# First q of block 0 through SP's hardware queue, k ahead of q in block 0, and state decay and transposes issued a block ahead

## The chip, the cores and the metric

The kernel runs on one core of a Trainium2 chip. The metric is the device time of one execution in microseconds (us), lower is better. Six runs of the kernel before gave a median of 243.56 us (242.32 to 244.79). One more execution was recorded by the hardware profiler; all times inside the kernel come from that trace. A core has these engines, each with its own instruction stream: TensorE (PE, matmuls; PEld is its weight load), Vector (DVE), Scalar (ACT), GpSimd (POOL) and Sync (SP). An engine runs its stream in order. DMAs are issued from a stream too: those of SP and Scalar through a hardware queue, those of GpSimd through a software queue that can also change the type of the data.

## The reference

Two stages. The first is attention with a decaying state. q, k and v have 4 batches, 8 heads, 768 positions and 64 values per head; `lam` has one decay factor per head, from 0.97 to 0.99. The second is a gated layer on the 3072 x 512 result.

```python
intra = np.einsum('bhic,bhjc->bhij', qb, kb) * Dmask[None]      # lam ** (i - j), below the diagonal
intra = np.einsum('bhij,bhjd->bhid', intra, vb)
inter = np.einsum('bhid,bhde->bhie', qb * lam_pow[None], kv_state)
out[:, :, sl] = intra + inter
kv_state = lam_block * kv_state + np.einsum('bhsd,bhse->bhde', kb * rev_pow, vb)
...
gate = 1.0 / (1.0 + np.exp(-(x @ w_gate)))
return (gate * (x @ w_val)) @ w_out                             # 512 -> 1536 -> 512
```

All inputs and the output are fp32.

## The kernel before

The positions are cut into NSTEP = 6 blocks of 128, and each block holds all 4 batches (numbered b) and 8 heads as 4 head pairs (hp, with u for one head of the pair). A block passes through attention and then through the gated layer, with its 4 x 128 = 512 tokens as the columns of a matmul.

The pieces of attention, for block n:

- `load` (L71) brings q, k or v of some batches with a DMA from GpSimd's queue that casts fp32 to bf16. A piece of one head and one position is 64 values: 256 bytes in HBM, 128 bytes after the cast.
- q and k are transposed. Blocks 0 and 1 do that on PE (`piece_tq0`, `piece_tk0`, `piece_t`); blocks 2 to 5 by two DMA transposes on SP's queue (`transpose_by_dma`, L147; results QR and KR). Vector multiplies the transposed q with the decay factors and gives QS (L162, L177, L186).
- `piece_s` (L206): the scores sp = k q on PE, for each batch in two banks of PSUM. `piece_m` (L214): Vector multiplies them with the mask and gives MT, one instruction for each u.
- `piece_a`: the output op, from the state Sb (L220, not for block 0) and from MT and v (L227); Scalar casts it to XT (L234), the input of the gated layer.
- `make_kd` (L238): GpSimd scales k by the reversed decay. `piece_c` (L246): PE multiplies that with v for the new part of the state, GpSimd scales the old state (sd, L251, four instructions for a block), and Vector adds both into Sb (L257, L259).

The gated layer: `piece_gv` does one tile of 128 of the 1536 columns: four matmuls to gp (L270), a sigmoid on Scalar (L273), four matmuls to vp (L276), and a product on Vector (L279, ht). `piece_gvh` does it for half of the tokens. `piece_po` does the last matrix for 128 tokens: 12 matmuls (L302), a copy by Scalar to ob (L305, four buffers), and a store of 256 KB on SP's queue (L306).

The order of the work is written out by hand: `manual_schedule` keeps for each engine the order in which the program issues its instructions, from L55 on. So the place of a call in the program sets what stands ahead of it in each engine's stream and queue. In the head, GpSimd issues q and k of batches 0 and 1, some index patterns, then q, k and v of the rest, and then the first three weight pairs. `idle` puts matmuls on zeros between the pieces of block 0. From L378 on, the pieces of attention of the next block lie between the tiles of the gated layer of the present one. The loads of block 2 and later come by `fetch` (L365): load, `make_kd` and the two transposes at one place, for block 2 after `t(1, 1)`, for block n + 1 at the start of iteration n of the loop at L422. Block 0's and block 1's `piece_po`, with their stores, stand ahead of that loop.

Buffers that matter: q, k and v have four each (blocks 0 to 3 take one each), kd two, sd four, QR and KR two, PSUM five banks for attention and three for the gated layer.

Of the kernel before, what the change touches and what calls it, by code (L numbers as in the profile page):

```python
# [8 lines left out]
FP32 = mybir.dt.float32  # L9
BF16 = mybir.dt.bfloat16  # L10
AF = mybir.ActivationFunctionType
ALU = mybir.AluOpType
# [4 lines left out]
def kernel(  # L17
# [11 lines left out]
    nc = tc.nc  # L29

    B, H, S, D = q.shape
    C = 128
    NSTEP = S // C
    HP = H // 2
# [22 lines left out]


    lam_bc = const.tile([128, H], FP32, tag="lam_bc")
    nc.sync.dma_start(out=lam_bc, in_=lam.partition_broadcast(128))  # L60

    WG = const.tile([128, NMT, DFF], BF16, tag="WG")
    WV = const.tile([128, NMT, DFF], BF16, tag="WV")
# [7 lines left out]
    def load(n, what, b0, b1):  # L71
        sl = slice(n * C, (n + 1) * C)
        for c in what:
            lst, src = {"q": (Q, q), "k": (K, k), "v": (V, v)}[c]
            if n not in lst:
                lst[n] = qkv.tile([128, B, H, D], BF16, tag=c + "b", name=c + "b")
            t = lst[n]
            nc.gpsimd.dma_start(  # L78
                out=t[:, b0:b1],
                in_=src[b0:b1, :, sl, :].rearrange("b h s d -> s (b h) d"))  # L80

    def load_gv(i, w):
        fs = slice(i * w, (i + 1) * w)
        nc.gpsimd.dma_start(out=WG[:, :, fs], in_=wg_r[:, :, fs])
        nc.gpsimd.dma_start(out=WV[:, :, fs], in_=wv_r[:, :, fs])
# [12 lines left out]
    nc.vector.memset(ident, 0.0)  # L98
    nc.vector.memset(tri, 0.0)

    load(0, "q", 0, 2)
    load(0, "k", 0, 2)
    for i, base in enumerate((-1, C - 1)):
        nc.gpsimd.iota(jn[:, i:i + 1], pattern=[[0, 1]], base=base, channel_multiplier=-1,
# [3 lines left out]
                   allow_small_or_imprecise_dtypes=True)  # L108
    nc.gpsimd.affine_select(out=tri, in_=tri, compare_op=ALU.is_gt, fill=1.0, base=0,
                            pattern=[[-1, C]], channel_multiplier=1)  # L110
    load(0, "q", 2, 4)
    load(0, "k", 2, 4)
    load(0, "v", 0, 2)
    load(0, "v", 2, 4)

    lnl = const.tile([128, H], FP32, tag="lnl")
    nc.scalar.activation(lnl, lam_bc, AF.Ln)
# [7 lines left out]
    for hp in range(HP):  # L125
# [4 lines left out]
    nc.scalar.activation(dec, lnp, AF.Exp, scale=float(C))  # L130
    nc.scalar.preload_act_table_set("sigmoid_and_others")
    mask = const.tile([128, 2, HP, C], FP32, tag="mask")
    nc.vector.tensor_tensor(out=mask, in0=tri.unsqueeze(1).unsqueeze(1).to_broadcast([128, 2, HP, C]),
                            in1=pk.rearrange("p (g u) -> p u g", u=2).unsqueeze(3).to_broadcast([128, 2, HP, C]),
                            op=ALU.mult)

    def idle(n, cols=TCH):
        w = ps_ff.tile([128, TCH], FP32, name="wm", tag="ff")
        for i in range(n):
            nc.tensor.matmul(w[:, :cols], lhsT=zero[:, :128], rhs=zero[:, :cols], start=True, stop=True,  # L140
                             skip_group_check=True)
# [14 lines left out]
    def piece_tq0(bp):  # L156
        tq = ps_at.tile([128, 2, HP, C], BF16, name="tq", tag="ps")
        for i in range(2):
            for hp in range(HP):
                nc.tensor.transpose(tq[:, i, hp, :], Q[0][:, 2 * bp + i, 2 * hp:2 * hp + 2, :], ident)  # L160
        QS[0, bp] = trsb.tile([128, 2, HP, C], BF16, tag="QS", name="QS")
        nc.vector.tensor_tensor(out=QS[0, bp], in0=tq,  # L162
                                in1=lamq.unsqueeze(1).to_broadcast([128, 2, HP, C]), op=ALU.mult)

    def piece_tk0(bp):
        tk = ps_at.tile([128, 2, HP, C], BF16, name="tk", tag="ps")
        for i in range(2):
            for hp in range(HP):
                nc.tensor.transpose(tk[:, i, hp, :], K[0][:, 2 * bp + i, 2 * hp:2 * hp + 2, :], ident)
        KS[0, bp] = trsb.tile([128, 2, HP, C], BF16, tag="KS", name="KS")  # L170
        for i in range(2):
            nc.scalar.copy(KS[0, bp][:, i], tk[:, i])
# [25 lines left out]
    def piece_s(n, bs):  # L198

        for b in bs:  # L200
# [7 lines left out]
                                     start=(hp == 0), stop=(hp == HP - 1), skip_group_check=True)  # L208
            SP[n, b] = sp

    def piece_m(n, b):
        MT[n, b] = mtp.tile([128, 2, HP, C], BF16, tag="MT", name="MT")
        for u in range(2):
            nc.vector.tensor_tensor(out=MT[n, b][:, u], in0=SP[n, b][u], in1=mask[:, u], op=ALU.mult)  # L214

    def piece_a(n, bs):
        for b in bs:
            OP[n, b] = ps_at.tile([128, HP, C], FP32, name="op", tag="ps")
            for hp in range(HP if n > 0 else 0):
                nc.tensor.matmul(OP[n, b][:, hp, :], lhsT=Sb[:, b, hp, :],  # L220
                                 rhs=QS[n, b // 2][:, b % 2, hp, :],
                                 start=(hp == 0), stop=False, skip_group_check=True)
        for b in bs:
            for hp in range(HP):
                for u in range(2):
                    us = slice(u * 64, (u + 1) * 64)
                    nc.tensor.matmul(OP[n, b][us, hp, :], lhsT=V[n][:, b, 2 * hp + u, :],  # L227
                                     rhs=MT[n, b][:, u, hp, :],
                                     start=(n == 0 and hp == 0), stop=(hp == HP - 1),
                                     skip_group_check=True)  # L230
        if n not in XT:
            XT[n] = xtp.tile([128, NMT, B, C], BF16, tag="XT", name="XT")
        for b in bs:
            nc.scalar.copy(XT[n][:, :, b, :], OP[n, b])  # L234

    def make_kd(n):
        KD[n] = kdp.tile([128, B, H, D], BF16, tag="kd", name="kd")
        nc.gpsimd.tensor_tensor(  # L238
            out=KD[n], in0=K[n],
            in1=kds.unsqueeze(1).unsqueeze(3).to_broadcast([128, B, H, D]), op=ALU.mult)  # L240

    def piece_c(n, bs):
        for b in bs:
            cp = ps_at.tile([128, HP, 128], FP32, name="cp", tag="ps")
            for hp in range(HP):
                nc.tensor.matmul(cp[:, hp, :], lhsT=KD[n][:, b, 2 * hp:2 * hp + 2, :],  # L246
                                 rhs=V[n][:, b, 2 * hp:2 * hp + 2, :],
                                 start=(hp == 0), stop=(hp == HP - 1), skip_group_check=True)
            if n > 0:
                sd = kdp.tile([128, HP, 128], FP32, tag="sd", name="sd", bufs=4)  # L250
                nc.gpsimd.tensor_tensor(out=sd, in0=Sb[:, b],  # L251
                                        in1=dec.unsqueeze(2).to_broadcast([128, HP, 128]),
                                        op=ALU.mult)
            for u in range(2):
                us = slice(u * 64, (u + 1) * 64)
                if n == 0:
                    nc.vector.tensor_copy(Sb[us, b, :, us], cp[us, :, us])  # L257
                else:
                    nc.vector.tensor_tensor(out=Sb[us, b, :, us], in0=cp[us, :, us],  # L259
                                            in1=sd[us, :, us], op=ALU.add)  # L260
# [48 lines left out]
    GW = DFF // 6  # L309
    for i in range(3):  # L310
        load_gv(i, GW)
    make_kd(0)
    load_gv(3, GW)
    load(1, "qk", 0, 2)
# [4 lines left out]
    load(1, "v", 2, 4)  # L319
    for i in range(3):  # L320
        load_wo(i, NFT // 3)
    make_kd(1)

    idle(10)
    piece_tq0(0)
    idle(4)
    piece_tk0(0)
    idle(2)
    piece_s(0, [0])
    piece_m(0, 0)  # L330
    piece_tq0(1)
    piece_s(0, [1])
    piece_m(0, 1)
    idle(3)
    piece_tk0(1)
    idle(2)
    piece_s(0, [2])
    piece_m(0, 2)
    piece_s(0, [3])
    piece_m(0, 3)  # L340
    nc.vector.memset(Sb, 0.0)
    piece_a(0, [0])
    piece_a(0, [1])
    idle(2)
    piece_a(0, [2])
    piece_a(0, [3])
    idle(2)

    def c(n, bp):
        piece_c(n, [2 * bp, 2 * bp + 1])  # L350
# [8 lines left out]
    def m(n, bp):  # L359
        piece_m(n, 2 * bp + 1)  # L360

    def a(n, bp):
        piece_a(n, [2 * bp, 2 * bp + 1])

    def fetch(n):  # L365
        load(n, "qkv", 0, B)
        make_kd(n)
        transpose_by_dma(n)

    def gv(n, *fts):  # L370
        for ft in fts:
            piece_gv(n, ft)
# [6 lines left out]
    c(0, 0)  # L379
    gv(0, 4)  # L380
    c(0, 1)
    gv(0, 5, 6, 7)
    t(1, 0)
    gv(0, 8)
# [4 lines left out]
    a(1, 0)  # L389
    gv(0, 11)  # L390
    t(1, 1)
    fetch(2)
    gvh(1, 0, 0, 1)
    sc(1, 1)
    gvh(1, 0, 2)
# [6 lines left out]
    c(1, 0)  # L402
    gv(1, 9)
    c(1, 1)
    gv(1, 10, 11)
    piece_po(0, 0)
    t(2, 0)
# [5 lines left out]
    sc(2, 1)  # L413
    m(2, 1)
    piece_po(0, 3)
    piece_po(1, 0)
    a(2, 0)
    piece_po(1, 1)
# [3 lines left out]
    for n in range(2, NSTEP):  # L422
        nx = n + 1
        if nx < NSTEP:
            fetch(nx)
            gv(n, 0)
            c(n, 0)
            gv(n, 1)
            c(n, 1)
            gv(n, 2)  # L430
            t(nx, 0)
            gv(n, 3)
            t(nx, 1)
            gv(n, 4)
            sc(nx, 0)
            gv(n, 5)
            m(nx, 0)
            gv(n, 6, 7)
            sc(nx, 1)
            gv(n, 8)  # L440
            m(nx, 1)
            a(nx, 0)
            gv(n, 9, 10, 11)
            a(nx, 1)
        else:
            gv(n, *range(NFT))
        for tt in range(B):
            piece_po(n, tt)
# [30 lines left out]
```

## Time and profile before

| | |
|---|---|
| median of 6 runs | 243.56 us (242.32 to 244.79) |
| the profiled execution | 243.52 us |
| its span (first to last instruction) | 241.3 us |
| PE busy | 224.8 us (93%) |
| Vector, Scalar, GpSimd busy | 105.7, 80.0, 85.0 us |
| data moved by DMA | 24.89 MB in 102289 packets |
| granted PE clock, mean | 0.985 of full |

Busy time is the time in which an engine works on an instruction; DMA issues, waits and branches do not count. The chain that ended last is followed back from the last instruction to what released it, and so on. A wait is put down to what ended it. Starts and lengths in the timeline are in us from the start of the span, and lines of the same kind are merged, with their number after the x. A view by windows gives the busy time of each engine in each stretch, the granted PE clock, and the busy share of the DMA engines (above 1 where more than one packet of an engine is under way).

### The profile page before, as it was taken

To read this page: it belongs to the slowest core of one execution; us is meant where nothing else is said; L and a number is where in the kernel's file an instruction comes from. 1 tells how busy PE (TensorE), PEld (TensorE's weight loads), DVE (VectorE), ACT (ScalarE), POOL (GpSimd) and SP (SyncE) were. 2 spreads that over 40 slices of the span, in tenths; PEclk is the share of its full clock that TensorE was granted. 3 is DMA by queue.
4 is the path that set the end of the run, shared out by engine and by line. 5 is a ranking of instruction groups with operands and counts; after the bars stand their busy time and mean duration, and the time that the engine had idled before them with its cause. 6 is when DMAs were issued, how large, how long until landed. Compare 5 with 4: busy or idle time off the path is not lost.

```text
span 241.3 us, 3816 instructions
## 1 busy us (share of the span) xinstructions
PE 224.8 (93%) x1528; PEld 115.9 (48%) x1553; DVE 105.7 (44%) x184; ACT 80.0 (33%) x145; POOL 85.0 (35%) x70
## 2 busy tenths in 40 slices
PE   7779999999999999929999999999999999999993
PEld 2444555886544555414554444554544554444441
DVE  2373855744647103545620298720397620243300
ACT  5453244444211333202432332432222431333221
POOL 8998650933972980892000085000000000000000
PEclk9999999999999999967999999999999999999999
DMA  8999999999999999999902480002650002200022
GB/s 52 143 180 197 174 184 167 207 152 155 142 97 186 180 93 195 162 154 156 86 3 87 128 134 3 0 3 87 152 112 1 0 3 87 87 0 0 3 87 87
DMA packets 102289, 24.89 MB, mean 103 GB/s; under 512 B 91520, under 2 KB 99200, under 8 KB 102272
## 3 DMA queue, kind: packets, MB, share of 16 engines
q0 software_dynamic: 82032, 14.16, 77.4%
q1 hardware_dynamic: 20240, 10.49, 19.4%
q8 instruction: 12, 0.20, 0.3%
q14 instruction: 5, 0.04, 0.0%
HBM read 28.32 MB, written 6.29 MB: 143 GB/s over the span
## 4 chain that ended last, share of the span: by engine, by line
PE 83%; DMA 6%; SPq 2%; DVE 2%; issue 2%; POOL 2%; ACT 1%; POOLq 0%; ACTq 0%; DVEq 0%
PE po L302 25%; PE vp L276 22%; PE gp L270 22%; DMA KR<-kb 3%; DMA kb<-in_k_dram 3%; PE sp L206 3%; PE vp L293 3%; PE op L227 3%; PE gp L287 2%; SPq L151 2%; PE op L220 2%; DVE MT L214 2%; PE cp L246 2%; POOL qb L78 1%; ACT ob L305 0%
## 5 line engine op out<-in xcount | busy, mean ns | idle before, releaser
L279 DVE TENSOR_TENSOR ht<-sg,vp 128x512 bf16<-128x512 bf16 x65 | 44.6, 687 | 94.2 <-PE vp L276 92.8
L270 PE MATMUL gp<-XT,WG 128*128 128x512 bf16 x249 | 66.1, 383 | 1.1 <-issue 0.5
L276 PE MATMUL vp<-XT,WV 128*128 128x512 bf16 x255 | 66.6, 382 | 0.3
L273 ACT ACTIVATE sg<-gp 128x512 bf16<-128x512 f32 x65 | 38.8, 597 | 81.0 <-PE gp L270 76.8
L302 PE MATMUL po<-WO,ht 128*128 128x512 bf16 x281 | 63.3, 379 | 0.9 <-DVE ht L279 0.5
L302 PEld LDWEIGHTS <-ht 128*128 128x128 bf16 x288 | 27.6, 98 | 33.7 <-issue 0.8
L238 POOL TENSOR_TENSOR kd<-kb,kds 128x2048 bf16<-128x2048 bf16 x6 | 21.8, 3630 | 58.1 <-PE cp L246 29.8
L276 PEld LDWEIGHTS <-WV 128*128 128x128 bf16 x260 | 25.6, 99 | 31.3 <-issue 1.1
L270 PEld LDWEIGHTS <-WG 128*128 128x128 bf16 x260 | 24.2, 98 | 27.6 <-issue 1.9
L214 DVE TENSOR_TENSOR MT<-sp,mask 128x512 bf16<-128x512 f32 x48 | 30.5, 683 | 8.4 <-PE sp L206 8.4
L305 ACT COPY ob<-po 128x512 f32<-128x512 f32 x24 | 14.1, 586 | 51.4 <-PE po L302 47.7
L251 POOL TENSOR_TENSOR sd<-Sb,dec 128x512 f32<-128x512 bf16 x16 | 17.0, 1089 | 0.0
L234 ACT CAST XT<-op 128x512 bf16<-128x512 f32 x24 | 13.0, 588 | 9.9 <-PE op L227 9.9
L259 DVE TENSOR_TENSOR Sb<-cp,sd 64x256 bf16<-64x256 f32 x32 | 13.5, 421 | 1.9 <-POOL sd L251 1.1
L78 POOL DMA_DIRECT2D qb<-in_q_dram x8 | 11.9, 1482 | 1.1 <-POOLq L463 0.8
L78 POOL DMA_DIRECT2D kb<-in_k_dram x8 | 11.4, 1426 | 1.1 <-DMA qb<-in_q_dram 1.1
L78 POOL DMA_DIRECT2D vb<-in_v_dram x8 | 11.4, 1427 | 0.6 <-DMA WG<-in_moe_w_gate_dram 0.6
L206 PE MATMUL sp<-QS,KR 64*128 64x128 bf16 x128 | 5.4, 228 | 5.6 <-DMA KR<-kb 5.2
L140 PE MATMUL wm<-zero 128*128 128x512 bf16 x23 | 8.1, 485 | 1.5 <-DVE zero L97 1.2
L177 DVE TENSOR_TENSOR QS<-QR,lamq 128x1024 bf16<-128x1024 bf16 x8 | 6.4, 796 | 5.8 <-DMA QR<-qb 5.8
L297 DVE TENSOR_TENSOR ht<-sg,vp 128x256 bf16<-128x256 bf16 x14 | 5.8, 419 | 6.1 <-PE vp L293 3.8
L293 PE MATMUL vp<-XT,WV 128*128 128x256 bf16 x56 | 8.4, 273 | 0.1
(51 smaller groups left out, 112.5 us busy)
## 6 DMA issues: line engine op xcount, KB each, us to landing
out_dram<-ob SPq DMA_DIRECT2D x24, 256.0 KB, 2.0
qb<-in_q_dram POOLq DMA_DIRECT2D x4, 512.0 KB, 8.1
kb<-in_k_dram POOLq DMA_DIRECT2D x4, 512.0 KB, 10.2
vb<-in_v_dram POOLq DMA_DIRECT2D x4, 512.0 KB, 13.0
WG<-in_moe_w_gate_dram POOLq DMA_DIRECT2D x6, 256.0 KB, 9.7
WV<-in_moe_w_val_dram POOLq DMA_DIRECT2D x6, 256.0 KB, 10.2
WO<-in_moe_w_out_dram POOLq DMA_DIRECT2D x3, 512.0 KB, 15.3
qb<-in_q_dram POOLq DMA_DIRECT2D x4, 256.0 KB, 7.7
```

The lines of the kernel that those rows point to most:

```text
L78: nc.gpsimd.dma_start(out=t[:, b0:b1], in_=src[b0:b1, :, sl, :].rearrange("b h s d -> s (b h) d"))
L214: nc.vector.tensor_tensor(out=MT[n, b][:, u], in0=SP[n, b][u], in1=mask[:, u], op=ALU.mult)
L238: nc.gpsimd.tensor_tensor(out=KD[n], in0=K[n], in1=kds.unsqueeze(1).unsqueeze(3).to_broadcast([128, B, H, D]), op=ALU.mult)
L251: nc.gpsimd.tensor_tensor(out=sd, in0=Sb[:, b], in1=dec.unsqueeze(2).to_broadcast([128, HP, 128]), op=ALU.mult)
L259: nc.vector.tensor_tensor(out=Sb[us, b, :, us], in0=cp[us, :, us], in1=sd[us, :, us], op=ALU.add)
L270: nc.tensor.matmul(gp, lhsT=WG[:, mt, fs], rhs=x[:, mt, :], start=(mt == 0), stop=(mt == NMT - 1))
L273: nc.scalar.activation(sg, gp, AF.Sigmoid)
L276: nc.tensor.matmul(vp, lhsT=WV[:, mt, fs], rhs=x[:, mt, :], start=(mt == 0), stop=(mt == NMT - 1))
L279: nc.vector.tensor_mul(HT[n, ft], sg, vp)
L293: nc.tensor.matmul(vp[:, cs], lhsT=WV[:, mt, fs], rhs=x[:, mt, cs], start=(mt == 0), stop=(mt == NMT - 1))
L302: nc.tensor.matmul(po, lhsT=HT[n, ft][:, tt * 128:(tt + 1) * 128], rhs=WO[:, ft, :], start=(ft == 0), stop=(ft == NFT - 1))
L305: nc.scalar.copy(ob, po)
```

## The change

- **lam** is loaded by Scalar's queue, no longer by SP's.
- **q of block 0, batches 0 and 1,** is loaded as fp32 by SP's hardware queue to a buffer of its own, qf, and cast by Vector to the place where it was, just ahead of the mask. GpSimd's queue starts with k of batches 0 and 1. k of batches 2 and 3 is loaded ahead of q of those, and v is cut into batches 0 to 2 and 3.
- **Block 0's pieces:** k of batches 2 and 3 is transposed ahead of q of those. QS comes in two instructions. Batch 2 uses `piece_m2`: Vector masks one half, and the other is copied to SBUF by Scalar and masked by GpSimd. XT of batches 2 and 3 is cast half by Vector, half by Scalar. The pieces stand ahead of `make_kd(0)` and the later loads, which moves that GpSimd product ahead of them in GpSimd's stream.
- **State decay:** the four sd of a block are issued by `fade` once the state before them is complete, right after `c` of the block before, no longer inside `piece_c` of their own block.
- **Blocks ahead:** `fetch` is taken apart. `make_kd(1)` follows the first `fade`. Block 3 is loaded after `c(1, 1)`, and its transposes are issued after `piece_po(0, 3)`. In the loop, iteration n loads block n + 2 after its `c(n, 1)`, and transposes it after `m(nx, 1)`.

```diff
-    nc.sync.dma_start(out=lam_bc, in_=lam.partition_broadcast(128))
+    nc.scalar.dma_start(out=lam_bc, in_=lam.partition_broadcast(128))
...
-    load(0, "q", 0, 2)
+    qf = const.tile([128, 2, H, D], FP32, tag="qf")
+    nc.sync.dma_start(out=qf, in_=q[0:2, :, 0:C, :].rearrange("b h s d -> s (b h) d"))
     load(0, "k", 0, 2)
...
+    Q[0] = qkv.tile([128, B, H, D], BF16, tag="qb", name="qb")
+    load(0, "k", 2, 4)
     load(0, "q", 2, 4)
-    load(0, "k", 2, 4)
-    load(0, "v", 0, 2)
-    load(0, "v", 2, 4)
+    load(0, "v", 0, 3)
+    load(0, "v", 3, 4)
...
+    nc.vector.tensor_copy(Q[0][:, 0:2], qf)
     nc.vector.tensor_tensor(out=mask, in0=tri.unsqueeze(1).unsqueeze(1).to_broadcast([128, 2, HP, C]),
...
-        nc.vector.tensor_tensor(out=QS[0, bp], in0=tq,
-                                in1=lamq.unsqueeze(1).to_broadcast([128, 2, HP, C]), op=ALU.mult)
+        for i in range(2):
+            nc.vector.tensor_tensor(out=QS[0, bp][:, i], in0=tq[:, i], in1=lamq, op=ALU.mult)
...
+    def piece_m2(n, b):
+        MT[n, b] = mtp.tile([128, 2, HP, C], BF16, tag="MT", name="MT")
+        nc.vector.tensor_tensor(out=MT[n, b][:, 0], in0=SP[n, b][0], in1=mask[:, 0], op=ALU.mult)
+        sc = const.tile([128, HP, C], FP32, tag="sc")
+        nc.scalar.copy(sc, SP[n, b][1])
+        nc.gpsimd.tensor_tensor(out=MT[n, b][:, 1], in0=sc, in1=mask[:, 1], op=ALU.mult)
...
-            nc.scalar.copy(XT[n][:, :, b, :], OP[n, b])
+            if n == 0 and b > 1:
+                nc.vector.tensor_copy(XT[n][:, 0:2, b, :], OP[n, b][:, 0:2])
+                nc.scalar.copy(XT[n][:, 2:4, b, :], OP[n, b][:, 2:4])
+            else:
+                nc.scalar.copy(XT[n][:, :, b, :], OP[n, b])
...
+    SD = {}
+
+    def fade():
+        for b in range(B):
+            SD[b] = kdp.tile([128, HP, 128], FP32, tag="sd", name="sd", bufs=4)
+            nc.gpsimd.tensor_tensor(out=SD[b], in0=Sb[:, b],
+                                    in1=dec.unsqueeze(2).to_broadcast([128, HP, 128]),
+                                    op=ALU.mult)
...
-            if n > 0:
-                sd = kdp.tile([128, HP, 128], FP32, tag="sd", name="sd", bufs=4)
-                nc.gpsimd.tensor_tensor(out=sd, in0=Sb[:, b],
-                                        in1=dec.unsqueeze(2).to_broadcast([128, HP, 128]),
-                                        op=ALU.mult)
+            sd = SD.pop(b, None)
...
+    idle(10)
+    piece_tq0(0)
+    idle(4)
+    piece_tk0(0)
+    idle(2)
+    piece_s(0, [0])
+    piece_m(0, 0)
+    piece_tk0(1)
+    piece_s(0, [1])
+    piece_m(0, 1)
+    idle(3)
+    piece_tq0(1)
+    idle(1)
+    piece_s(0, [2])
+    piece_m2(0, 2)
+    piece_s(0, [3])
+    piece_m(0, 3)
+    piece_a(0, [0])
+    piece_a(0, [1])
+    idle(3)
+    piece_a(0, [2])
+    piece_a(0, [3])
+    nc.vector.memset(Sb, 0.0)
+    idle(1)
+
     make_kd(0)
     load_gv(3, GW)
     load(1, "qk", 0, 2)
...
-    make_kd(1)
-
-    idle(10)
...
-    def fetch(n):
-        load(n, "qkv", 0, B)
-        make_kd(n)
-        transpose_by_dma(n)
...
     c(0, 1)
+    fade()
+    make_kd(1)
     gv(0, 5, 6, 7)
...
-    fetch(2)
+    load(2, "qkv", 0, B)
+    make_kd(2)
+    transpose_by_dma(2)
...
     c(1, 1)
+    load(3, "qkv", 0, B)
+    fade()
+    make_kd(3)
     gv(1, 10, 11)
...
     piece_po(0, 3)
+    transpose_by_dma(3)
     piece_po(1, 0)
...
-            fetch(nx)
             gv(n, 0)
             c(n, 0)
             gv(n, 1)
             c(n, 1)
+            if n + 2 < NSTEP:
+                load(n + 2, "qkv", 0, B)
+                fade()
+                make_kd(n + 2)
+            elif nx < NSTEP - 1:
+                fade()
...
             m(nx, 1)
+            if n + 2 < NSTEP:
+                transpose_by_dma(n + 2)
             a(nx, 0)
```

More of the change, by code (lines that the diff above doesn't have):

```diff
@@ L321 @@
         load_wo(i, NFT // 3)
-    make_kd(1)
-    idle(10)
[L325 to L347, printed above, removed]
     def c(n, bp):
```

## The prediction

> **What bounds the kernel now.** I read the busy times first: TensorE (PE) is busy for 224.8 of 241.3 us, so a gain can only come from where PE waits. The list of waits, for PE alone and for Vector, names the candidates (us in total, times, longest):
>
> ```profile
> PE sp L206 <- DMA KR<-kb: 5.2, 1, 5.2
> DVE Sb L259 <- POOL sd L251: 1.1, 1, 1.1
> ```
>
> One wait of 5.2 us stands out: the score matmuls of one block wait for the transposed k. To price it I cut the trace at the first gate matmul of loop iterations 2, 3 and 4, which do the same work on PE:
>
> ```profile
> core 0: us, PE busy (x) PEld busy (x) DVE busy (x) ACT busy (x) POOL busy (x), PEclk, DMA share, GB/s
> 92.37:135.17 42.80, 37.25 (x238) 18.33 (x241) 17.27 (x30) 11.66 (x20) 12.66 (x8) 0.92 1.29 116
> 135.17:170.71 35.54, 35.18 (x237) 17.56 (x240) 18.07 (x30) 11.65 (x20) 8.50 (x5) 1.00 0.26 60
> 170.71:206.24 35.53, 35.21 (x237) 17.55 (x240) 17.32 (x30) 11.66 (x20) 0.00 (x0) 1.00 0.25 60
> ```
>
> Iteration 2 is 7.26 us longer than the two others (42.80 - 35.54), with a granted clock of 0.92. The chain that ended last shows how (start, length, what):
>
> ```profile
> 93.23 0.33 SPq L306
> ...
> 93.65 5.50 SPq L151
> ...
> 99.24 8.01 DMA KR<-kb
> 107.25 0.05 issue
> 107.30 1.03 PE sp L206 x16
> 108.33 1.82 PE gp L270 x4
> ```
>
> The transposes of block 3 start only at 93.65, right behind an output store (L306); KR lands at 107.25. The stall also cools PE: the next four gate matmuls take 1.82 us where a full clock gives 0.86. SP's queue in time shows why they start there:
>
> ```profile
> 71.17 22.39 SPq L306 DMA_DIRECT2D out_dram<-ob  x8
> 93.65 5.50 SPq L151 DMA_TRANSPOSE QR<-qb  x1
> 99.24 5.91 SPq L151 DMA_TRANSPOSE KR<-kb  x1
> 136.26 2.09 SPq L151 DMA_TRANSPOSE QR<-qb  x1
> ```
>
> All eight stores of blocks 0 and 1 stand ahead of them, although block 3's k was there by 77.06 (kd of block 3 starts then on GpSimd). In iterations 3 and 4 nothing waits for the transposes.
>
> The second place is the head. The first gate matmul starts at 17.78, and the head's last transposes wait for a load:
>
> ```profile
> 0.74 0.40 SPq L60 DMA_DIRECT2D lam_bc<-in_lam_dram  x1
> 1.27 1.32 POOL L78 DMA_DIRECT2D qb<-in_q_dram  x1 [0.82 <-POOLq L463]
> 6.34 0.62 PE L160 MATMUL tq<-ident,qb 128*128 128x128 bf16 x8 [0.81 <-DMA qb<-in_q_dram]
> 8.63 0.62 PE L169 MATMUL tk<-ident,kb 128*128 128x128 bf16 x8 [0.81 <-DMA kb<-in_k_dram]
> 12.45 0.62 PE L169 MATMUL tk<-ident,kb 128*128 128x128 bf16 x8 [0.22 <-DMA kb<-in_k_dram]
> 17.78 1.02 PE L270 MATMUL gp<-XT,WG 128*128 128x512 bf16 x4
> ```
>
> The loads land at 6.3, 8.6, 10.5, 12.4: one 256 KB load per 1.9 us once data flows. Cut into single us, the DMA share is 0.05 in 2 to 3 us, 0.59 in 3 to 4, 2.00 after.
>
> **Transposes a block ahead.** Block 3's load moves ahead of the fade on GpSimd, and its two transposes ahead of block 1's four stores on SP. GpSimd: the load was issued at 65.6 behind four sd (4.02 us); now it follows kd of block 2, which ends at 61.7, about 4 us earlier. Its k took 9.5 us to land, so about 71 to 73. SP: the transposes follow the fourth store, whose copy starts at 79.97, so about 80.6 in the old times; less 2.1 us of earlier gains, 78.5. The slowest seen (5.5 issue and 12.0 to landing for QR, then 8.0 for KR from its own issue) put QR at 90.5 and KR at 92. They are needed at about 98 (QS on Vector) and 100 (sp on PE), so 6 us or more is spare and the whole 7.26 us goes; I book 7.2. Behind the transposes on SP now wait block 1's stores, for up to 11 us. The four ob buffers make this free: their next users are the copies of block 2's outputs, at 127 in the old times. The transposes of 4 and 5 stand ahead of the stores of 2 and 3 likewise, and their loads will have landed. What is late next in iteration 2 is nothing: iterations 3 and 4 leave PE idle for about 0.3 us in all.
>
> **Fade a block ahead.** The four sd of each block are the same instructions, earlier. Only block 1's were late: Vector waited 1.1 us, and its queued ht kept an output bank, so PE lost 0.78 us in 60.44 to 67.77 (7.33 less 6.55 busy) where the same stage of block 2 loses 0.05 (6.10 less 6.05). That gives 0.7. On GpSimd, fade now stands ahead of kd of the block to come and waits for Vector's Sb; kd and the load behind it wait too. For block 1: weight loads are issued by about 34.9, fade 4.1 us, done by 39; kd of block 1 waited for its k until 41.87 anyway. For blocks 3 to 5, kd and loads are tens of us from use. Cost 0; without that cover it would be the 4.1 us. Sums under way on GpSimd at the same time slowed one QS from 0.68 to 1.33 us in iteration 3 without lengthening it: 0.
>
> **Head: the load.** qf takes the place of lam at the head of SP's queue (0.74); lam's 4 KB took 2.5 us to land, and lam on Scalar puts 0.40 us before a table load that ends at 2.0 while lam lands at 3.2: free. qf is 512 KB. No row shows a fp32 load with 256-byte pieces. By written bytes at the rates of the trace (195 GB/s for weights, 141 for q and k) it takes 2.7 to 3.7 us after lam's 2.5: landed at 5.9 to 6.9. By pieces (2048, as q's, 1.9 us) 5.1. I take 6.4, nearest to the weights' rate with k's first load beside it. The Trainium skill, "DMA: Bandwidth & Descriptors", section "Issuing engines are not separate DMA queues", speaks against a gain here: all queues interleave on the same 16 engines, and another issuer saves sequencer time only. Against it stands the row of the DMA share: those engines were empty until 3 us. By the rule and written bytes, the load starts about 1.3 us earlier but is 0.8 to 1.8 longer, so the rest comes 0.5 us later to 0.5 earlier; k being first in GpSimd's queue and the empty engines alone would give a whole slot, 1.9. Both ends stay; I take 1.2 earlier.
>
> **Head: the sequence on Vector.** From qf's landing: cast, mask 1.2, QS 0.7, scores 0.4, four MT 2.6, QS 0.7, handoff 0.3, one MT 0.65, two MT 1.3, op 0.4, XT 0.6. The cast has no row: the fp32 mask of the same shape is 1.23 us; the skill's "VectorE: DVE Perf Modes", section "The perf-mode tier table", has a fp32 copy at two elements a cycle, 1.227 us for 2048 and so about 0.7, as an estimate, for 1024. The mask has two inputs and the cast one, but I keep 1.2 as the row; by the rule the head is 0.5 shorter. Sum 10.0, so gp at 6.4 + 10.0 = 16.4: 1.4 us earlier. The split of block 0's third MT takes 0.65 off Vector and adds a Scalar copy (0.59) and a GpSimd product, nearest sd, 1.03, done at about 14.5, when Vector's last MT ends: no wait. It pushes kd of block 0 (13.69) and the fourth weight pair about 1 us later; DMA has work queued until 22 or later, so nothing starves. XT halves on two engines save about 0.3, inside the sum; QS in two halves adds an overhead of about 0.1. Sb's memset (0.91) goes behind XT, before a Vector that idles 2 us: 0. Last, data must keep pace: WV's first piece landed at 18.2 for a use at 18.64, block 1's k at 41.76 for a use at 42.5. With loads 1.2 us earlier PE may come 1.6 and 1.9 earlier, so 1.4 holds. Ends: -0.8 (a loss) to 2.2.
>
> **Sum.** 7.2 + 0.7 + 1.4 = 9.3 us off the profiled execution's own 243.52 (span 241.3 and 2.2 around it, taken as unchanged; the median is 243.56): 234.2 us.
>
> **Rivals.**
> A: qf lands at 7.8 or later, so the head gives nothing: 243.5 - 7.9 = 235.6, and 237 with qf at 9.2. For it: 256-byte pieces and k beside it; against: the empty engines.
> B: block 3's load, now issued 4 to 5 us earlier, collides with block 2's transposes. KR of 2 was issued at 59.74 and landed 7.1 later, for a use at 73.04; shifted, issued at 58.3 and needed at 70.9. It would need over 12.6 us; the slowest seen took 12.0. If it misses by 3 us, the time is 237.2.
> C: the transposes of 3 still come late since block 4's load now runs beside them from 75 on. They would need 21 us where the slowest pair took 13.6; half the stall left gives 237.8, all of it 241.4 and more.
> D, slower than before: the hardware queue makes 2048 short pieces so slowly that block 0 waits for qf. From a landing of 7.8 on, each us costs one; past 15.7 (7.9 us of other gains used up) the kernel is slower. That is 512 KB in 15 us, 35 GB/s, a quarter of the slowest steady rate seen. Landing at 18 gives 235.6 + 10.2 = 245.8, a cold PE on top not counted.
>
> **Numbers.** Forecast 0.69 (232.8 to 235.4); A 0.14; B 0.06; C 0.04; D 0.07. A measurement can tell about 0.5%, 1.2 us, from no change. Of D, 0.02 (qf landing from 14.5 to 16.9) lies within that. So faster 0.93, same 0.02, slower 0.05. Range 232.8 to 237.2: head at its best below; A and B's first us above.
>
> **What would show it.** Right: the wait of sp for KR gone, block 3's QR issued near 78, iteration 2 at 35.5 with clock 1.00; PE's loss at c of block 1 near 0.05; the first gp near 16.4, tq at 7.7 or before. Wrong: a new wait on KR or QR of block 2 near 71, gp waiting for WV, or tq after 9.

## The result, and the profile after

The kernel after takes 243.37 us (median of 33 runs, 238.71 to 245.34), the kernel before 243.41 us (median of 70, 241.69 to 245.56). A ratio of the faster executions alone, which leaves out 25 of the 33 runs of the kernel after, is 0.991 (95% interval 0.9883 to 0.9938). The gain is therefore between nothing and 1.2%, where 9.3 us (3.8%) were forecast.

The profiled execution took 241.48 us (span 239.3), 1.9 us less than the kernel's own median. The sums below are made inside it: 2.0 us off the span of before, 241.3.

The waits of PE in the profile after (columns: who waited, at what line, for whom; us in total, times, longest):

```profile
PE sp L209 <- DVE QS L180: 2.8, 1, 2.8
PE gp L289 <- DVE ht L298: 2.4, 2, 1.2
PE tq L163 <- DVE qb L135: 2.2, 1, 2.2
```

The wait for KR is gone, as forecast. In its place PE waits for Vector three times after the head, 5.2 us in all, and 2.2 us in the head for the cast of q. Two rows of the page's costliest groups say what has become slow on Vector; first before, then after (busy in all, mean ns of one):

```profile
L177 DVE TENSOR_TENSOR QS<-QR,lamq 128x1024 bf16<-128x1024 bf16 x8 | 6.4, 796 | 5.8 <-DMA QR<-qb 5.8
```

```profile
L180 DVE TENSOR_TENSOR QS<-QR,lamq 128x1024 bf16<-128x1024 bf16 x8 | 14.8, 1851 | 0.0
```

The same eight instructions cost 8.4 us more. The view by windows, cut at the same pieces of work as before (head to the first gp, to the first cp of block 1, to the first po, and to the first gp of iterations 2 to 5), shows where this counts:

```profile
core 0: us, PE busy (x) PEld busy (x) DVE busy (x) ACT busy (x) POOL busy (x), PEclk, DMA share, GB/s
0.00:18.57 18.57, 13.85 (x119) 7.26 (x122) 9.60 (x18) 9.19 (x21) 14.24 (x22) 0.91 2.08 148
18.57:61.44 42.87, 42.53 (x350) 27.13 (x354) 24.58 (x46) 17.87 (x35) 32.02 (x25) 1.00 1.91 172
61.44:67.51 6.07, 6.02 (x40) 3.24 (x40) 5.26 (x11) 1.79 (x3) 6.07 (x5) 1.00 1.57 153
67.51:94.65 27.14, 24.19 (x175) 11.98 (x177) 9.55 (x11) 6.25 (x11) 12.28 (x8) 1.00 2.12 161
94.65:131.62 36.97, 35.44 (x237) 17.55 (x240) 20.41 (x30) 11.66 (x20) 13.14 (x8) 1.00 1.27 140
131.62:168.59 36.97, 35.40 (x236) 17.56 (x240) 20.41 (x30) 11.66 (x20) 8.10 (x5) 1.00 0.26 58
168.59:204.13 35.54, 35.22 (x238) 17.55 (x241) 17.32 (x30) 11.66 (x20) 0.00 (x0) 1.00 0.08 31
```

| stage | before | after | difference | forecast |
|---|---|---|---|---|
| head, to the first gp | 17.78 | 18.57 | +0.8 | -1.4 |
| to c of block 1 | 42.87 | 42.87 | 0 | 0 |
| c of block 1, to the first po | 7.12 | 6.07 | -1.05 | -0.7 |
| po of blocks 0 and 1 | 24.60 | 27.14 | +2.54 | 0 |
| iteration 2 | 42.80 | 36.97 | -5.83 | -7.2 |
| iteration 3 | 35.54 | 36.97 | +1.43 | 0 |
| iteration 4 | 35.53 | 35.54 | 0 | 0 |
| the rest | 35.06 | 35.17 | +0.1 | 0 |

The row of before for the po stage:

```profile
67.77:92.37 24.60, 24.18 (x173) 11.98 (x176) 6.71 (x11) 6.25 (x11) 15.63 (x10) 1.00 1.55 152
```

Iterations 2 and 3 are now alike, 36.97, and both are 1.43 longer than iteration 4; the po stage lost 2.54. These three stages have GpSimd work, and iteration 4 has none (0.00 in the POOL column). The timeline around each QS of the first two stages (start, length, what; in brackets the idle time before it and its releaser):

```profile
74.67 3.62 POOL L252 TENSOR_TENSOR kd<-kb,kds 128x2048 bf16<-128x2048 bf16 x1 [3.55 <-DMA kb<-in_k_dram]
75.62 3.22 DVE L180 TENSOR_TENSOR QS<-QR,lamq 128x1024 bf16<-128x1024 bf16 x1
...
78.89 0.62 PE L209 MATMUL sp<-QS,KR 64*128 64x128 bf16 x16 [2.79 <-DVE QS L180]
...
102.67 4.07 POOL L252 TENSOR_TENSOR kd<-kb,kds 128x2048 bf16<-128x2048 bf16 x1
...
103.78 3.50 DVE L180 TENSOR_TENSOR QS<-QR,lamq 128x1024 bf16<-128x1024 bf16 x1
107.21 0.68 DVE L298 TENSOR_TENSOR ht<-sg,vp 128x512 bf16<-128x512 bf16 x1
107.94 1.02 PE L289 MATMUL gp<-XT,WG 128*128 128x512 bf16 x4 [1.21 <-DVE ht L298]
```

In the kernel before, kd stood clear of QS at the same two places:

```profile
75.88 0.68 DVE L177 TENSOR_TENSOR QS<-QR,lamq 128x1024 bf16<-128x1024 bf16 x1
77.06 3.62 POOL L238 TENSOR_TENSOR kd<-kb,kds 128x2048 bf16<-128x2048 bf16 x1 [6.33 <-PE sp L206]
...
97.16 3.61 POOL L238 TENSOR_TENSOR kd<-kb,kds 128x2048 bf16<-128x2048 bf16 x1 [7.43 <-DMA kb<-in_k_dram]
...
105.64 0.69 DVE L177 TENSOR_TENSOR QS<-QR,lamq 128x1024 bf16<-128x1024 bf16 x1 [5.75 <-DMA QR<-qb]
```

QS takes 0.68 us where nothing runs beside it. In the kernel after it starts about 1 us after kd and ends 0.55 us after kd's end (78.84 against 78.29; 107.28 against 106.74). That looks like a wait for kd, and not like a slower run. In the po stage sp stands behind it. In iterations 2 and 3 the ht behind it on Vector comes late, and with it the output bank that the next gp needs.

### The profile page after: what moved, and what is told of

The parts are those of the page before. It is cut to its first block, busy times and chain, and to the rows that moved or that the text cites. A ratio compares the mean times of both kernels' runs of the same rounds, so it can differ in the third digit from the quotient of the medians.

```text
span 239.3 us, 3824 instructions
## 1 busy us (share of the span) xinstructions
PE 223.7 (93%) x1527; PEld 116.2 (49%) x1552; DVE 115.4 (48%) x188; ACT 80.2 (34%) x146; POOL 85.8 (36%) x70
## 4 chain that ended last, share of the span: by engine, by line
PE 89%; DVE 5%; DMA 2%; issue 1%; ACT 1%; DVEq 0%
PE po L321 25%; PE gp L289 24%; PE vp L295 23%; PE op L237 3%; PE sp L209 3%; PE vp L312 3%; PE gp L306 2%; DMA qf<-in_q_dram 2%; PE cp L269 2%; PE op L230 2%; DVE MT L224 2%; DVE QS L180 1%; PE wm L143 1%; DVE qb L135 1%; DVE ht L298 1%
## 5 line engine op out<-in xcount | busy, mean ns | idle before, releaser
L289 PE MATMUL gp<-XT,WG 128*128 128x512 bf16 x249 | 65.2, 379 | 3.9 <-DVE ht L298 2.4
L224 DVE TENSOR_TENSOR MT<-sp,mask 128x512 bf16<-128x512 f32 x46 | 29.2, 682 | 6.8 <-PE sp L209 6.8
L252 POOL TENSOR_TENSOR kd<-kb,kds 128x2048 bf16<-128x2048 bf16 x6 | 22.6, 3768 | 14.1 <-DMA kb<-in_k_dram 14.1
L180 DVE TENSOR_TENSOR QS<-QR,lamq 128x1024 bf16<-128x1024 bf16 x8 | 14.8, 1851 | 0.0
L248 ACT CAST XT<-op 128x512 bf16<-128x512 f32 x22 | 11.8, 589 | 8.7 <-PE op L237 8.6
L278 DVE TENSOR_TENSOR Sb<-cp,sd 64x256 bf16<-64x256 f32 x32 | 13.5, 421 | 0.8
L78 POOL DMA_DIRECT2D qb<-in_q_dram x7 | 10.5, 1506 | 0.0
L143 PE MATMUL wm<-zero 128*128 128x512 bf16 x22 | 8.6, 533 | 1.4 <-DVE zero L97 1.2
L306 PE MATMUL gp<-XT,WG 128*128 128x256 bf16 x56 | 8.4, 273 | 0.0
```

Source lines behind the costliest of these rows:

```text
L78: nc.gpsimd.dma_start(out=t[:, b0:b1], in_=src[b0:b1, :, sl, :].rearrange("b h s d -> s (b h) d"))
L180: nc.vector.tensor_tensor(out=QS[n, bp], in0=QR[n][:, 2 * bp:2 * bp + 2], in1=lamq.unsqueeze(1).to_broadcast([128, 2, HP, C]), op=ALU.mult)
L252: nc.gpsimd.tensor_tensor(out=KD[n], in0=K[n], in1=kds.unsqueeze(1).unsqueeze(3).to_broadcast([128, B, H, D]), op=ALU.mult)
L289: nc.tensor.matmul(gp, lhsT=WG[:, mt, fs], rhs=x[:, mt, :], start=(mt == 0), stop=(mt == NMT - 1))
```

## Theories

**H:** the change removes the KR stall as forecast, but it puts kd of blocks 3, 4 and 5 onto the moment at which Vector does QS. Vector and GpSimd get in each other's way over SBUF, and QS lasts until kd is done. The Trainium skill, "SBUF — State Buffer", section "Who interferes with whom", states such a rule: a Vector instruction with two SBUF inputs contends with a GpSimd instruction that reads SBUF, and the later one is blocked until the first is done. QS has both inputs in SBUF, and kd reads k from SBUF; MT and ht have one input in PSUM, and beside kd they kept their 0.67 to 0.69 us.

**The rivals:** that the transposes of a block ahead, moved beside the loads, make QS late or slow through the DMA engines; that the new head shifts everything, so that the collision comes from the head; and that QS is slow for a reason of its own (where its operands lie), whatever GpSimd does.

## The experiments

**The kernel after once more** (no edit), for the spread beside the others.

> The changed kernel once more, unaltered, to see how wide its times spread. Theory H (Vector's QS of two SBUF inputs waits for a GpSimd product under way): the stall at QS of block 2 depends on whether kd of block 3 begins before it, so the span falls into groups: about 236.7 where kd comes after QS, 239.3 where it comes before, and about 241.3 where the 2.8 us stall also cools PE. Rival (the spread is noise of the chip that has nothing to do with QS): the stage from the first po of block 0 to the end of iteration 1's po is about 27.1 us whatever the time.

Measured: 243.18 us (239.09 to 245.41, 12 runs), 0.9922 (0.9886 to 0.9959). The profile again has the wait for QS, 3.0 us, and QS of block 2 at 3.42. So the stalls came again in a second traced execution. The three groups that were expected are not clear in the spans: one run at 237.1, three at 239.1 to 239.3, and eight spread from 240.2 to 243.3. With one traced execution in each set of runs the stated rival, that the spread has nothing to do with QS, stays untested.

**kd behind QS.** A one-column copy on GpSimd that reads QS holds kd of blocks 3 to 5 until the second QS of the block before is done. Loads, fade and transposes stay where the change put them.

```diff
+    def kd_after(n, m):
+        gt = kdp.tile([128, 1], BF16, tag="gt", name="gt", bufs=2)
+        nc.gpsimd.tensor_copy(gt, QS[m, 1][:, 0, 0, 0:1])
+        make_kd(n)
...
     fade()
-    make_kd(3)
...
     t(2, 1)
+    kd_after(3, 2)
...
                 fade()
-                make_kd(n + 2)
...
             t(nx, 1)
+            if n + 2 < NSTEP:
+                kd_after(n + 2, nx)
```

> The changed kernel, with kd of blocks 3, 4 and 5 held on GpSimd until the second QS of the block before is written. Theory H: the po stage of blocks 0 and 1 falls from 27.1 to about 24.6 us, iterations 2 and 3 from 36.97 to 35.54 each, every QS is below 1.3 us, and the time falls by 5.4 us or more against the changed kernel, to about 236. Rival (QS is slow since transposes, loads or stores write SBUF at that time): QS stays at 3.2 to 3.5 us and the time does not move, 241.5 to 243.4.

Measured: 236.32 us (236.23 to 236.41, 4 runs), 0.9728 (0.97 to 0.9755). The timeline of Vector and GpSimd at the same two places, and the same three stages by windows:

```profile
76.20 0.68 DVE L180 TENSOR_TENSOR QS<-QR,lamq 128x1024 bf16<-128x1024 bf16 x1
...
77.08 3.62 POOL L252 TENSOR_TENSOR kd<-kb,kds 128x2048 bf16<-128x2048 bf16 x1
...
101.82 0.68 DVE L180 TENSOR_TENSOR QS<-QR,lamq 128x1024 bf16<-128x1024 bf16 x1
...
103.07 3.62 POOL L252 TENSOR_TENSOR kd<-kb,kds 128x2048 bf16<-128x2048 bf16 x1 [0.32 <-PE sp L209]
```

```profile
68.09:92.69 24.60, 24.35 (x177) 11.98 (x176) 7.54 (x11) 6.24 (x11) 12.95 (x9) 1.00 1.88 163
92.69:128.23 35.54, 35.54 (x242) 17.51 (x241) 17.75 (x30) 11.65 (x20) 12.92 (x9) 1.00 1.57 157
128.23:163.76 35.53, 35.53 (x241) 17.58 (x240) 17.75 (x30) 11.65 (x20) 7.82 (x6) 1.00 0.27 60
```

QS is 0.68 again, and the stages are 24.60, 35.54 and 35.53: what the change lost there (2.54 + 1.43 + 1.43 = 5.4 us) comes back with one moved instruction per block. (The span falls by 4.8 only, 239.3 to 234.5, because the first gp came at 19.15 in this execution, 0.6 later.) The longest QS left is one of 1.37 beside the sd, where less than 1.3 was expected. The rivals of the DMA engines and of the operands fall: transposes, loads and operands are as in the kernel after. This is H's main test. It shows that QS waits for kd; that the two meet in SBUF is the page's reason, for which the runs have only that MT and ht, with an input in PSUM, keep their time beside kd.

**The head of before under the rest of the change.**

```diff
-    nc.sync.dma_start(out=qf, in_=q[0:2, :, 0:C, :].rearrange("b h s d -> s (b h) d"))
+    load(0, "q", 0, 2)
...
-    nc.vector.tensor_copy(Q[0][:, 0:2], qf)
...
-    piece_m2(0, 2)
+    piece_m(0, 2)
```

(With these go the order of the loads and pieces of block 0, lam's queue, QS in one instruction and XT on Scalar.)

> The changed kernel with the whole head of the kernel before (q of block 0 by GpSimd's queue, lam by SP, the order of k and q, mask and XT as before), blocks ahead and fade as changed. If the new head costs 0.8 us by itself (18.57 against 17.78 at the first gate matmul), the time is 0.8 us below the changed kernel, and the granted clock of the head is 1.00 again. If a cold PE in the head costs more later, 2 us or more below.

Measured: 242.84 us (241.06 to 244.51, 12 runs), 0.9992 (0.9963 to 1.0021). The first gp starts at 17.73, as before; QS takes 3.65 and PE waits 3.2 for it. So the head is not its cause: the collision is there without it.

**The new head alone,** on the kernel before.

```diff
+    nc.sync.dma_start(out=qf, in_=q[0:2, :, 0:C, :].rearrange("b h s d -> s (b h) d"))
-    load(0, "q", 0, 2)
...
+    nc.vector.tensor_copy(Q[0][:, 0:2], qf)
...
-    piece_m(0, 2)
+    piece_m2(0, 2)
```

> The kernel before with only the changed head. If the head is a loss of 0.8 us, 244.3 us, with the wait for KR of block 3 (about 7 us) still there; if the prediction's sum of the head was right and only the surroundings hid it, 242.1 us.

Measured: 244.47 us (242.54 to 245.32, 12 runs), 1.0054 (1.0028 to 1.008). The first gp starts at 19.58, and the wait for KR is still there:

```profile
PE sp L209 <- DMA KR<-kb: 4.9, 1, 4.9
```

The head by itself is a loss of 1.3 us in the median (244.47 against 243.15). It is not the same in each execution: in the six traces that have this head with ten fillers the first gp starts at 18.40 to 19.62, so the 18.57 of the table is near the better end; with the head of before, four traces have 17.73 to 18.00.

**The head of before with kd behind QS:** the edits of the two kernels above (head of before, and `kd_after`) together.

> The changed kernel with kd of blocks 3 to 5 held back as in gate, and the head of the kernel before. If head and blocks ahead are independent and add up, the first gate matmul is at about 17.75 instead of 19.15 us (gate's trace) and the time is 1.4 us below gate, 234.9 us. If the later head was hidden anyway by block 1's loads, the time is as gate's, 236.3.

Measured: 235.22 us (234.93 to 235.23, 5 runs), 0.9679 (0.9648 to 0.971); first gp at 17.79. Against 236.32 with the new head this puts the new head's loss at 1.1 us in a kernel without stalls (runs of before beside them: 243.03 and 243.15).

**kd in four parts,** one for each batch, left where the change put it. If a Vector instruction waits for the GpSimd instruction under way, it should now wait for a part only.

```diff
-        nc.gpsimd.tensor_tensor(
-            out=KD[n], in0=K[n],
-            in1=kds.unsqueeze(1).unsqueeze(3).to_broadcast([128, B, H, D]), op=ALU.mult)
+        for b in range(B):
+            nc.gpsimd.tensor_tensor(
+                out=KD[n][:, b], in0=K[n][:, b],
+                in1=kds.unsqueeze(2).to_broadcast([128, H, D]), op=ALU.mult)
```

> The changed kernel with each kd as four GpSimd instructions, one for each batch, nothing held back. Theory H in its sharp form (QS waits for the one GpSimd instruction under way, and gets in between two): QS at most 0.9 + 0.55 = 1.5 us, the stall at block 2 goes and the time falls to 236.3 to 237.5. Rival (Vector and GpSimd share by time, so that QS stays slow as long as kd runs): QS stays above 3 us and the time at 241 to 243.

Measured: 236.77 us (234.97 to 237.36, 6 runs), 0.9736 (0.9696 to 0.9776). The time is less telling than it looks: in this trace kd of block 3 began only in the last quarter of a us of QS (77.11, against a QS from 76.67 to 77.35), and kd of block 4 a full us after QS, at 104.03, so no QS had to wait there. Only iteration 3 tests it:

```profile
136.72 4.94 POOL L253 TENSOR_TENSOR kd<-kb,kds 128x512 bf16<-128x512 bf16 x4
...
137.83 0.93 DVE L180 TENSOR_TENSOR QS<-QR,lamq 128x1024 bf16<-128x1024 bf16 x1
```

QS started 1.1 us into kd, as in the kernel after, and took 0.93 instead of 3.50: it got in between two parts, and kd became longer, 4.94. The iteration took 35.53. One overlap is a single case, but it is as H has it: the wait lasts as long as the one GpSimd instruction. That kd of 3 and 4 began late here also shows how near the collision stands to not happening: its start hangs on when k lands.

**Transposes a block ahead, and nothing else:** the kernel before, with `fetch` taken apart, but its decay and its head as they were. The lines with `load` and `make_kd` only keep GpSimd's order as it was: between the old place and the new one there is no other GpSimd instruction. What moves is the place of the transposes on SP.

```diff
     c(1, 1)
+    load(3, "qkv", 0, B)
+    make_kd(3)
...
     piece_po(0, 3)
+    transpose_by_dma(3)
...
-            fetch(nx)
...
             c(n, 1)
+            if n + 2 < NSTEP:
+                load(n + 2, "qkv", 0, B)
+                make_kd(n + 2)
...
             m(nx, 1)
+            if n + 2 < NSTEP:
+                transpose_by_dma(n + 2)
```

> The kernel before with only the order of the transposes changed: those of block 3 ahead of block 1's stores, those of 4 and 5 ahead of the stores of 2 and 3; loads, kd and sd keep GpSimd's order of before, and the head is that of before. If the late transposes alone made the 7.26 us stall, iteration 2 falls from 42.8 to 35.5 us and the time to 236.2. If Theory H holds, kd of block 4 (97.2 to 100.8 before) now meets QS of block 3, which no longer waits for its transposes: QS about 2.5 us, iteration 2 between 35.5 and 37, the time 236.2 to 237.6.

Measured: 236.9 us (236.5 to 238.74, 6 runs), 0.9723 (0.9685 to 0.9761). This one part of the change is worth 7.2 us by medians (244.09 to 236.9) and 6.9 by spans (241.3 to 234.4), more than the whole. One collision that costs time is left, in iteration 2:

```profile
99.31 3.94 POOL L238 TENSOR_TENSOR kd<-kb,kds 128x2048 bf16<-128x2048 bf16 x1 [10.24 <-DVE ht L279]
100.33 3.46 DVE L177 TENSOR_TENSOR QS<-QR,lamq 128x1024 bf16<-128x1024 bf16 x1
```

It makes that iteration 36.47. In the po stage kd starts at 76.39, after that QS (75.16, 0.68), and in iteration 3 it began 2.8 us ahead of QS (132.72 against 135.55), which took 1.33 and lengthened nothing (35.54). GpSimd's order is that of before, so a collision needs neither the moved load nor the moved fade: QS, which no longer waits for QR, starts at 100.33 instead of 106.84, and kd of block 4 starts later, at 99.31 instead of 97.16, as its k took 13.5 us to land where it had taken 10.7. The change as a whole adds two shifts. Block 3's load ahead of the fade brings kd of block 3 forward to 74.67 and onto QS; and the fade ahead of kd, which waits for Vector's Sb, holds kd of block 5 back to 139.64, close ahead of QS.

**A warm head.** In the head of the kernel after, PE runs out of filler matmuls before the cast is done, and its granted clock is 0.50 from 9.4 to 11.3 us. This kernel has kd behind QS and 18 fillers ahead of tq, and drops the four between tq and tk.

```diff
-    idle(10)
+    idle(18)
     piece_tq0(0)
-    idle(4)
     piece_tk0(0)
```

> Gate, with 18 instead of 10 filler matmuls ahead of block 0's first transposes and none between those of q and those of k. Theory P (the head is late since PE waits cold for qf's cast, and the fillers then stand at half clock between tq and tk): tk at about 8.4 us instead of 10.5, the clock full, the first gate matmul at 16.8 to 17.3, the time 1.8 to 2.3 us below gate, about 234.3. Rival (Vector's chain of cast, mask, QS and MT sets the head): the first gate matmul moves by less than 0.7 us.

Measured: 234.39 us (234.35 to 234.47, 5 runs), 0.9649 (0.9618 to 0.968). First the head of the kernel after in the timeline, then that of this one:

```profile
0.75 0.46 SPq L102 DMA_DIRECT2D qf<-in_q_dram  x1
...
5.85 2.43 POOL L78 DMA_DIRECT2D vb<-in_v_dram  x2
...
6.26 1.53 DVE L135 CAST qb<-qf 128x1024 bf16<-128x1024 f32 x1 [4.91 <-DMA qf<-in_q_dram]
...
7.85 0.62 PE L163 MATMUL tq<-ident,qb 128*128 128x128 bf16 x8 [2.23 <-DVE qb L135]
...
8.31 1.34 PE L143 MATMUL wm<-zero 128*128 128x512 bf16 x4
...
9.44 1.06 PE L172 MATMUL tk<-ident,kb 128*128 128x128 bf16 x8
...
18.57 1.02 PE L289 MATMUL gp<-XT,WG 128*128 128x512 bf16 x4 [0.71 <-ACT XT L246]
```

```profile
7.84 0.62 PE L163 MATMUL tq<-ident,qb 128*128 128x128 bf16 x8 [0.45 <-DVE qb L135]
...
8.30 0.61 PE L172 MATMUL tk<-ident,kb 128*128 128x128 bf16 x8
...
17.05 1.02 PE L294 MATMUL gp<-XT,WG 128*128 128x512 bf16 x4 [0.40 <-ACT XT L246]
```

tq starts at the same 7.85, but tk follows 1.1 us earlier and takes 0.61 instead of 1.06, and the first gp comes 1.5 us earlier, at 17.05. The granted clock is 1.00 from 7.4 to 9.0 us. Against the kernel with kd behind QS, from which this one is made, the first gp is 2.1 us earlier (19.15) and the median 1.9 us lower. Whether the longer row of fillers or the missing four did it was not separated. Against the head of before with kd behind QS (235.22 us, first gp at 17.79) the new head is now a gain of 0.8 us; the head of before with more fillers was not tried. This is the quickest version of all.

**The cast, twice:** kd behind QS, and the same cast once more in the last block, near 204 us, where GpSimd does nothing. Nobody uses its result.

```diff
+            gv(n, 0, 1)
+            cq = const.tile([128, 2, H, D], BF16, tag="cq")
+            nc.vector.tensor_copy(cq, qf)
```

> Gate, with the cast of qf done once more to an unused buffer in the last block, when GpSimd is idle. If the cast of the head is slow (1.53 us) because GpSimd issues DMAs at the same time, the second one takes about 0.7 us; if the cast just is as slow as a fp32 instruction of that size, 1.2 to 1.5.

Measured, one execution: 236.83 us, and

```profile
6.29 1.50 DVE L135 CAST qb<-qf 128x1024 bf16<-128x1024 f32 x1 [4.93 <-DMA qf<-in_q_dram]
...
203.98 0.69 DVE L483 CAST cq<-qf 128x1024 bf16<-128x1024 f32 x1
```

The cast itself is 0.69 us; in the head 0.8 us are added. In all seven traces with the v loads issued beside it the cast took 1.50 to 1.54.

**The cast without GpSimd beside it:** the warm head with 16 fillers, and the loads of v of block 0 held on GpSimd until the cast is done.

```diff
-    load(0, "v", 0, 3)
-    load(0, "v", 3, 4)
...
     nc.vector.tensor_copy(Q[0][:, 0:2], qf)
+    gq = const.tile([128, 1], BF16, tag="gq")
+    nc.gpsimd.tensor_copy(gq, Q[0][:, 0, 0, 0:1])
+    load(0, "v", 0, 3)
+    load(0, "v", 3, 4)
```

> Gate_warm, with v of block 0 issued on GpSimd only once qf is cast (16 fillers ahead of tq). If the cast takes 1.5 us since it waits for the DMA issue under way on GpSimd, it falls to 0.7 and tq starts at about 7.0 instead of 7.8; v lands about 1 us later, so the first gate matmul moves by no more than 0.5 us either way. If the cast is slow for another reason, such as DMA writes, it stays at 1.5.

Measured: 234.8 us (234.42 to 235.54, 6 runs), 0.963 (0.9594 to 0.9665), and

```profile
6.08 0.69 DVE L133 CAST qb<-qf 128x1024 bf16<-128x1024 f32 x1 [4.73 <-DMA qf<-in_q_dram]
```

So the 0.8 us come with GpSimd's issue of the v loads (from 5.85 on in the kernel after), and not from the cast being the first of its kind. The end does not come earlier by it: tq starts at 7.35, as the fillers ran until then, and v comes late instead (PE's op waits 1.1 us for vb); the first gp is at 17.31, against 17.05 with the warm head.

## Why the prediction was wrong

**Transposes a block ahead: right about the wait.** QR of block 3 was issued at 83.31 and KR at 90.10, about 5 us later than booked, and no PE wait for them was left; the booked 6 us to spare took that up. With kd out of the way iteration 2 is 35.54, 7.26 us less than before. But "What is late next in iteration 2 is nothing" was wrong by itself: with only the transposes moved, QS met kd there, and the iteration took 36.47, 0.9 us more.

**Fade a block ahead, c of block 1: right.** Booked 0.7, measured 1.05. PE's idle time there fell from 0.78 to 0.05 us as forecast; the other 0.3 lies in the busy time of the same 40 matmuls (6.34 to 6.02), which nothing here explains.

**Fade a block ahead, the work on GpSimd: the step that failed.** It read "For blocks 3 to 5, kd and loads are tens of us from use. Cost 0", and "Sums under way on GpSimd at the same time slowed one QS from 0.68 to 1.33 us in iteration 3 without lengthening it: 0". I asked when kd's result is needed, and not what runs beside it; and I took the 1.33 for the size of a cost without looking at what was under way. It was kd; the sd began only at 143.19. The timeline of before at that place has it:

```profile
139.61 3.61 POOL L238 TENSOR_TENSOR kd<-kb,kds 128x2048 bf16<-128x2048 bf16 x1 [29.79 <-PE cp L246]
...
142.44 1.33 DVE L177 TENSOR_TENSOR QS<-QR,lamq 128x1024 bf16<-128x1024 bf16 x1
143.19 4.92 POOL L251 TENSOR_TENSOR sd<-Sb,dec 128x512 f32<-128x512 bf16 x4
144.29 0.92 DVE L177 TENSOR_TENSOR QS<-QR,lamq 128x1024 bf16<-128x1024 bf16 x1
```

This QS ended at 143.77, 0.55 us after kd's end at 143.22: the same wait with the same tail as in the kernel after, and short only because QS began 0.8 us before kd's end. A QS that begins at the start of kd would, by this row, last until 0.55 us after 3.6. The change brings the two together from both sides, kd by its new place and QS by its earlier start, and the kernel with kd behind QS shows the price: 5.4 us. No rival named this.

**Head, the load: right for qf, half right for the rest.** The cast could start at 6.26 (booked 6.4). The loads behind it were booked 1.2 us earlier: k of batches 0 and 1 landed at 7.97 instead of 8.6, and the last of q and k at 11.6 instead of 12.4, so 0.6 to 0.8 (the estimate by interleaving queues had ended at 0.5).

**Head, the sequence: wrong by 2.2 us** (18.57 in place of 16.4; up to 3.2 in the other traces of this head). Two terms were off. The cast, booked at 1.2, took 1.53 beside GpSimd and 0.69 alone: the rule that was put aside, a fp32 copy at two elements a cycle (the Trainium skill, "VectorE: DVE Perf Modes", section "The perf-mode tier table", about 0.7 as an estimate), comes out for the instruction alone, 0.69; the rest of the 1.53 is again GpSimd. The larger term was left out: the sum followed Vector alone. PE idled 2.23 us ahead of tq; the four fillers between tq and tk then took 1.34 us (four such matmuls take 0.86 at a full clock), and tk 1.06 against 0.61. The warm head took 1.5 us off at an unchanged tq. The 0.65 us that still lie between 17.05 and the booked 16.4 contain the 0.3 of the cast. In that trace PE also waits 0.75 us, at its first op, for v of block 0, which landed at 14.33 and stands nowhere in the sum; no run removed that wait.

**The sum** had 9.3 us. In the profiled execution: 7.26 and 1.05 gained, 5.4 given back by kd beside QS (1.43 of it inside iteration 2), 0.8 lost in the head, 0.1 elsewhere: 2.0. Of the rivals, A (the head gives nothing) happened in part, by another way than a late qf; B, C and D did not.

**What stays open.** The median of the kernel after lies 1.9 us above its profiled execution, so some of its runs lose more than this sum shows. Kernels in which PE stalls by about 2.8 us or more (before, after, either head without kd behind QS) spread over 2.8 to 6.6 us; the three with kd behind QS and v in its place over 0.3 us at most; the others over 1.1 to 2.4. By medians kd behind QS is worth 6.9 us (243.18 to 236.32), by its stages 5.4. The rest may be the clock after a stall: of the 20 runs of the kernel after above 243 us, 19 have a mean granted clock of 0.978 to 0.985, where the profiled one has 0.989, and 0.006 of 240 us is 1.4 us, as an estimate. Which stage loses it is not shown, since none of these runs was traced.

## What to carry to other kernels

When an instruction moves, ask what will run beside it, and not only when its result is due: a 3.6 us GpSimd product that nobody waits for cost 0.9 to 2.5 us in each stage where it began about 1 us ahead of a Vector instruction on the way to PE. A single odd duration in the trace of before (0.68 become 1.33) is a mechanism showing itself; price it with the longest instruction that can stand in that place. And a gain at the start of a chain is a gain only if each engine of the chain is ready: count PE's fillers and their place along with Vector's steps.

## What the runs showed of the hardware

- A bf16 product on Vector with both inputs in SBUF (QS), begun during a GpSimd product (kd or sd), ended about 0.55 us after the end of a GpSimd product in all traces, and so took up to 3.65 us behind kd, five times its own 0.68. With one input in PSUM (MT, ht) a Vector product kept its 0.67 to 0.69 us beside kd.
- GpSimd waits too: kd that began while a QS was under way took 4.07 us instead of 3.62 (both times in the kernel after).
- It is not only computing on GpSimd that delays Vector: beside the issue of DMAs from GpSimd's queue a fp32 to bf16 cast took 0.8 us longer (1.50 to 1.54, against 0.69 and 0.69).
- Cutting the GpSimd product into four let Vector in after one part (0.93 us), and beside the sd, four instructions of about 1.03 us, a QS took 0.69 to 1.60 in all traces but one. But a row of short instructions is no safe gap: in the last kernel above, a QS that began 0.35 us into the sd took 3.24 and ended 0.55 us after the third of them. What decides that was not tried.
- In the head of the kernel after, ten fillers on zeros took 4.43 us (0.44 each), then PE idled 2.23 us, and the transposes tk took 1.06 us. With 18 fillers (6.20 us, 0.34 each), an idle time of 0.45 and no fillers between tq and tk they took 0.61. In the kernel before, ten fillers and an idle time of 0.81 left the first transposes of q and of k at 0.62.
